# The first expert layer in quarters of the array's columns, with h turned in 32x32 squares on VectorE

## The chip, the cores and the metric

The kernel runs on one core of one Trainium2 chip. The metric is the device time of one execution in microseconds, as the median of several runs. The engines have short names in the profile: PE is TensorE (matmuls), PEld its weight loads, DVE is VectorE, ACT is ScalarE, POOL is GpSimd, SP is SyncE. PSUM is the memory that matmuls write to, SBUF the one they read from.

## What is computed

The first part is attention in chunks of 64, over 8 batches of 8 heads with 576 tokens of 64 numbers; the change does not touch it. Its output is seen as x with N = 4608 rows (tokens) of D = 512 numbers. Then each token goes to one of E = 8 experts, and this is where the change lies:

```python
xn = x / (np.linalg.norm(x, axis=-1, keepdims=True) + 1e-06)
en = expert_emb / (np.linalg.norm(expert_emb, axis=-1, keepdims=True) + 1e-06)
logits = xn @ en.T / tau
expert_idx = np.argmax(logits, axis=1)
...   # gate_w: the softmax weight of the chosen expert
for e in range(E):
    mask = expert_idx == e
    ...
    h = np.maximum(x[mask] @ w1[e], 0.0)          # 512 -> 1024
    out[mask] = gate_w[mask, None] * (h @ w2[e])  # 1024 -> 512
```

Everything is fp32.

## The kernel before

After attention and routing, the tokens are sorted by expert and worked through in steps of 128. A step holds two groups of G = 64 tokens, and each group (`s` = 0, 1) belongs to one expert, with weights of its own in SBUF (`w1_sb[s]`, `w2_sb[s]`, two buffers each). There are NT = 36 steps that always run, and up to 4 more under a condition, of which one runs with this input.

A matmul contracts over the 128 partitions: `lhsT` is loaded into the array, `rhs` streams past it, and the output lies in PSUM with one partition for each column of `lhsT`. A `lhsT` of 64 columns fills half of the array's columns, so the two groups run beside each other in the two halves. The name `tile(..., tag=..)` takes a buffer from a pool; a pool has `bufs` buffers for each tag, and a new tile of that tag waits until the last reader of the tile that had the buffer is done. The instructions of an engine are issued in the order of the program (`manual_schedule`).

```python
P, CH, G = 128, 64, 64; KD = D // P      # 4
KF = F // P                              # 8
ctx.enter_context(tc.manual_schedule())
...
with (
    tc.tile_pool(name="blk", bufs=2) as bp,
    tc.tile_pool(name="ps_x", bufs=1, space=PSUM) as ps_x,
    tc.tile_pool(name="ps_h", bufs=3, space=PSUM) as ps_h,
    tc.tile_pool(name="ps_ht", bufs=2, space=PSUM) as ps_ht,
    tc.tile_pool(name="ps_y", bufs=2, space=PSUM) as ps_y,
):
    ...

def turn_xb(j):
    t = xin.pop(j)
    ps = ps_x.tile([P, KD, P], FP32, tag="x", name="x_ps")
    for c in range(KD):
        nc.tensor.transpose(ps[:, c], t[:, c * P : c * P + P], ident)
    xT = bp.tile([P, KD, P], FP32, tag="xbT", name="xbT")
    nc.vector.tensor_copy(xT, ps)
    mo[j] = {"xT": xT, "xin": t}

def hidden(j):
    d = mo[j]
    h = bp.tile([P, F], FP32, tag="h", name="h")
    for fh in range(F // 512):
        ps = ps_h.tile([P, 512], FP32, tag="h", name="h_ps")
        for c in range(KD):
            for s in range(2):
                nc.tensor.matmul(
                    ps[G * s : G * s + G],
                    lhsT=d["xT"][:, c, G * s : G * s + G],
                    rhs=w1_sb[s][j % 2][:, c, fh * 512 : fh * 512 + 512],
                    start=(c == 0),
                    stop=(c == KD - 1),
                )
        dst = h[:, fh * 512 : fh * 512 + 512]
        if fh % 2:
            nc.scalar.activation(dst, ps, AF.Relu)
        else:
            nc.vector.tensor_scalar(dst, ps, 0.0, None, ALU.max)
    d["h"] = h

def turn_h(j):
    d = mo[j]
    hT = bp.tile([P, KF, P], FP32, tag="hT", name="hT")
    for g in range(KF // 4):
        ps = ps_ht.tile([P, 4, P], FP32, tag="ht", name="ht_ps")
        for c in range(4):
            f0 = (4 * g + c) * P
            nc.tensor.transpose(ps[:, c], d["h"][:, f0 : f0 + P], ident)
        if g % 2:
            nc.scalar.copy(hT[:, 4 * g : 4 * g + 4], ps)
        else:
            nc.vector.tensor_copy(hT[:, 4 * g : 4 * g + 4], ps)
    d["hT"] = hT

def result(j):
    d = mo.pop(j)
    ps = ps_y.tile([P, D], FP32, tag="y", name="y_ps")
    for c in range(KF):
        for s in range(2):
            nc.tensor.matmul(
                ps[G * s : G * s + G],
                lhsT=d["hT"][:, c, G * s : G * s + G],
                rhs=w2_sb[s][j % 2][:, c],
                start=(c == 0),
                stop=(c == KF - 1),
            )
    y = bp.tile([P, D], FP32, tag="y", name="y", bufs=3)
    nc.scalar.activation(y, ps, AF.Copy, scale=d["gate"])
    ...   # y goes to its rows of out by an indirect DMA
```

`hidden` makes h with tokens on the partitions and the 1024 features along the row. The second layer contracts over features, so it needs h turned, with features on the partitions: `turn_h` does this with eight 128x128 transposes on TensorE into PSUM, and two copies to SBUF give `hT`. `gates(j)` (not shown) makes the gate weight on ScalarE and VectorE. The order of the steps is this:

```python
load_w1(0)
load_w1(1)
load_w2(0)
load_w2(1)
turn_xb(0)
hidden(0)
load_w1(2)
gates(0)
turn_xb(1)
gates(1)

LEAST = NT
for j in range(LEAST + 1):
    if j + 1 < LEAST:
        hidden(j + 1)
        if j + 3 < NST:
            load_w1(j + 3)
    if j < LEAST:
        turn_h(j)
    if j + 2 < LEAST:
        turn_xb(j + 2)
        gates(j + 2)
    if j > 0:
        result(j - 1)
        if j + 1 < NST:
            load_w2(j + 1)
    if j + XBUF < NST:
        gather_x(j + XBUF)
        if j + XBUF + 1 < NST:
            gather_spot(j + XBUF + 1)

steps = number(n_steps, NST, ENG.PE, ENG.DVE, ENG.Activation, ENG.Pool, ENG.SP)

def more(j):
    with tc.If(steps > j):
        turn_xb(j)
        hidden(j)
        if j + 2 < NST:
            load_w1(j + 2)
        turn_h(j)
        gates(j)
        result(j)
        if j + 2 < NST:
            load_w2(j + 2)
        if j + 1 < NST:
            more(j + 1)

more(LEAST)
```

## Time and profile before

| | before |
|---|---|
| time, median of 3 runs | 806.37 us (802.37 to 807.18) |
| span of the profiled execution | 810.2 us |
| TensorE busy | 743.9 us, 92% of the span |
| ScalarE, VectorE busy | 290.7 us (36%), 251.7 us (31%) |
| h matmuls (L635) | 1184 records, 267.9 us busy |
| y matmuls (L668) | 1184 records, 262.0 us busy |
| turning of h (L656) | 296 records, 40.6 us busy |
| turning of x (L604) | 148 records, 22.8 us busy |

The profile shows one execution. An fp32 matmul leaves two records, so a step has 32 records for 16 h matmuls; 37 steps make 1184. The page cuts the span into 40 slices, each with a digit for the busy share of an engine in tenths; PEclk is the clock that TensorE was granted, in tenths of full speed. A group's line has the source line, the engine, the operation, output and inputs with their shapes, the count, then busy time and mean length of one in ns, then the idle time of the engine before them and what ended it. Attention and routing take up the first 200 us or so, and the expert steps run from about 210 us to the end.

### The profile page before, as it was taken

What the parts mean: (1) busy time and instruction counts of PE and PEld (TensorE: products, weight loads), DVE (VectorE), ACT (ScalarE), POOL (GpSimd) and SP (SyncE); (2) the same over time, 40 slices, a digit from 0 to 9 for tenths busy, and PEclk for the clock granted to TensorE, in tenths of its full rate; (3) what the DMA queues carried; (4) which work ended last, traced back from release to release, by engine and by line L of the source; (5) the groups of instructions that cost most, each with busy time, mean ns of one, the idle gap of its engine ahead of it and who ended that gap; (6) DMA issues with size and microseconds to landing.
All of it is one profiled execution on the core that took longest, in us unless ns stands there. A gap on an engine that the chain in (4) does not pass through costs nothing.

```text
span 810.2 us, 15342 instructions
## 1 busy us (share of the span) xinstructions
PE 743.9 (92%) x6033; PEld 367.7 (45%) x6033; DVE 251.7 (31%) x703; ACT 290.7 (36%) x520; POOL 221.3 (27%) x270
## 2 busy tenths in 40 slices
PE   2799999985569999999999999999999999999994
PEld 2688888874124333343343333343333343333331
DVE  2467777775221121121121121121121122122100
ACT  3345455441142243243243243333334334334102
POOL 4235556545420211211211311311211221221220
PEclk9999999995778999999999999999999999999998
DMA  9999999993670100115583416688530444312140
GB/s 177 234 264 246 238 251 234 258 399 133 233 247 1 51 27 27 53 59 202 189 305 131 155 61 229 253 328 323 169 118 27 144 144 131 140 44 79 72 150 9
DMA packets 117739, 132.37 MB, mean 163 GB/s; under 512 B 79860, under 2 KB 83252, under 8 KB 117664
## 3 DMA queue, kind: packets, MB, share of 16 engines
q1 hardware_dynamic: 101136, 84.18, 35.9%
q0 software_dynamic: 16528, 47.17, 18.4%
q8 instruction: 49, 0.80, 0.4%
q14 instruction: 26, 0.21, 0.1%
HBM read 383.07 MB, written 21.80 MB: 500 GB/s over the span
## 4 chain that ended last, share of the span: by engine, by line
PE 83%; DMA 4%; issue 3%; DVE 3%; SPq 3%; POOL 1%; ACT 0%; POOLq 0%; DVEq 0%; ACTq 0%
PE y_ps L668 31%; PE h_ps L635 29%; PE ht_ps L656 4%; PE rt_ps L288 4%; PE pv L255 3%; PE tr L280 3%; PE tr L199 3%; PE sc L215 2%; SPq L188 2%; PE tr L241 2%; PE x_ps L604 2%; DMA w<-in_moe_w_dram 2%; DMA spot<-spots,src_row 1%; DVE x L266 1%; SPq L176 1%
## 5 line engine op out<-in xcount | busy, mean ns | idle before, releaser
L635 PE MATMUL h_ps<-w,xbT 128*64 128x512 f32 x1184 | 267.9, 604 | 9.9 <-DMA w<-in_moe_w_dram 6.6
L668 PE MATMUL y_ps<-w,hT 128*64 128x512 f32 x1184 | 262.0, 595 | 0.0
L635 PEld LDWEIGHTS h_ps<-w,xbT 128*64 128x64 f32 x1184 | 88.5, 140 | 181.3 <-issue 174.4
L677 POOL DMA_INDIRECT out_dram<-y,spot x37 | 37.8, 1022 | 441.6 <-ACT y L676 425.7
L668 PEld LDWEIGHTS y_ps<-w,hT 128*64 128x64 f32 x1184 | 81.8, 137 | 154.6 <-issue 154.1
L644 ACT ACTIVATE h<-h_ps 128x512 f32<-128x512 f32 x37 | 22.1, 597 | 259.2 <-PE h_ps L635 231.8
L646 DVE TENSOR_SCALAR h<-h_ps 128x512 f32<-128x512 f32 x37 | 25.6, 691 | 225.4 <-PE h_ps L635 225.4
L676 ACT ACTIVATE y<-y_ps,gate 128x512 f32<-128x512 f32 x37 | 25.4, 687 | 126.1 <-PE y_ps L668 126.1
L660 DVE COPY hT<-ht_ps 128x512 f32<-128x512 f32 x37 | 25.6, 692 | 126.9 <-PE ht_ps L656 123.5
L623 ACT ACT_TABLE_LOAD x37 | 47.5, 1283 | 0.7
L618 ACT ACT_TABLE_LOAD x37 | 47.5, 1283 | 0.7
L527 POOL DMA_INDIRECT xin<-x_rows,spot x40 | 41.4, 1034 | 22.2 <-issue 11.3
L656 PEld LDWEIGHTS ht_ps<-ident,h 128*128 128x128 f32 x296 | 31.7, 141 | 30.4 <-issue 29.2
L282 ACT COPY xT<-tr 128x512 f32<-128x512 f32 x36 | 21.1, 586 | 64.8 <-PE tr L280 46.1
L527 POOL DMA_INDIRECT spot<-spots,src_row x40 | 40.4, 1009 | 13.9 <-issue 11.6
L288 PE MATMUL rt_ps<-enT,xT 128*128 128x8 f32 x288 | 37.6, 257 | 5.8 <-DVE m L310 5.7
L199 PE MATMUL tr<-ident,kx 128*128 128x128 f32 x144 | 24.2, 296 | 18.4 <-DMA kx<-in_k_dram 18.4
L288 PEld LDWEIGHTS rt_ps<-enT,xT 128*128 128x128 f32 x288 | 37.5, 203 | 7.7 <-DVE m L310 4.1
L656 PE MATMUL ht_ps<-ident,h 128*128 128x128 f32 x296 | 40.6, 280 | 0.1
L176 POOL DMA_DIRECT2D qx<-in_q_dram x40 | 35.3, 886 | 19.0 <-PE tr L199 17.8
L372 POOL DMA_INDIRECT spots<-m,dest x36 | 36.7, 1019 | 11.4 <-issue 10.6
L273 POOL DMA_DIRECT2D x_rows<-x x36 | 20.3, 565 | 70.0 <-DVE x L266 55.8
(123 smaller groups left out, 659.3 us busy)
## 6 DMA issues: line engine op xcount, KB each, us to landing
w<-in_moe_w_dram SPq DMA_DIRECT2D x160, 2048.0 KB
v<-in_v_dram SPq DMA_DIRECT2D x64, 144.0 KB
x_rows<-x POOLq DMA_DIRECT2D x36, 256.0 KB
qx<-in_q_dram POOLq DMA_DIRECT2D x32, 256.0 KB
kx<-in_k_dram SPq DMA_DIRECT2D x32, 256.0 KB
w<-in_moe_w_dram POOLq DMA_DIRECT2D x4, 2048.0 KB
spots<-empty SPq DMA_DIRECT2D x1, 2312.0 KB
qx<-in_q_dram POOLq DMA_DIRECT2D x8, 128.0 KB
```

The lines of the kernel that those rows point to most:

```text
L176: eng.dma_start(out=x[done : done + n], in_=src[b, :, s : s + n, :].rearrange("h p d -> p h d"),)
L199: nc.tensor.transpose(ps[:, i], a[:, i * P : i * P + P], ident)
L288: nc.tensor.matmul(rt_ps[:, 0, batch_of[t][1]], lhsT=d["xT"][:, c], rhs=enT[:, c], start=(c == 0), stop=(c == KD - 1),)
L372: ins = nc.gpsimd.indirect_dma_start(out=spots, out_offset=bass.IndirectOffsetOnAxis(ap=at, axis=0), in_=m, in_offset=None, bounds_check=S ...
L527: nc.gpsimd.indirect_dma_start(out=dst, out_offset=None, in_=table, in_offset=bass.IndirectOffsetOnAxis(ap=at, axis=0), bounds_check=rows - 1,
L618: nc.scalar.activation(rn, rn, AF.Sqrt)
L623: nc.scalar.activation(sh, sh, AF.Exp, accum_out=gate)
L635: nc.tensor.matmul(ps[G * s : G * s + G], lhsT=d["xT"][:, c, G * s : G * s + G], rhs=w1_sb[s][j % 2][:, c, fh * 512 : fh * 512 + 512], sta ...
L646: nc.vector.tensor_scalar(dst, ps, 0.0, None, ALU.max)
L656: nc.tensor.transpose(ps[:, c], d["h"][:, f0 : f0 + P], ident)
L668: nc.tensor.matmul(ps[G * s : G * s + G], lhsT=d["hT"][:, c, G * s : G * s + G], rhs=w2_sb[s][j % 2][:, c], start=(c == 0), stop=(c == KF ...
L677: ins = nc.gpsimd.indirect_dma_start(out=out, out_offset=bass.IndirectOffsetOnAxis(ap=spot[:, j, E : E + 1].bitcast(I32), axis=0), in_=y, ...
```

## The change

It makes h in another arrangement, so that the turning for the second layer needs no TensorE. A transpose on VectorE turns 32x32 squares, each in its place: of a square of 32 partitions by 32 elements, rows become columns, but the square does not move to other partitions. So h has to lie such that each square is already on the partitions that its features need. The new `hidden` takes 32 tokens at a time as `lhsT`, in one of four quarters of the array's columns. Quarter `r` (32 columns) computes, for these 32 tokens, the features whose number modulo 128 lies in 32r to 32r + 31: it reads w1 in pieces of 32 columns, one from each 128. Its output is on partitions 32r to 32r + 31. Each square then holds 32 tokens by 32 features on the partitions where hT wants those features, and one VectorE transpose for each half of the tokens writes hT. Relu is done by ScalarE alone on the way from PSUM to SBUF.

A step has 64 matmuls of 256 columns in place of 16 of 512 columns, and no transposes or copies for h. `turn_h` goes; its work stands at the end of `hidden`. PSUM buffers that it used go to x (2 in place of 1) and h (4 in place of 3). The buffers of the SBUF tiles stay as they were: two each for `xbT`, `h` and `hT`, where an `h` tile now holds half a step.

```diff
--- before.py
+++ after.py
@@ -46,6 +46,7 @@
     NT = N // P
     NCB = S // CH
     G = P // 2
+    Q = 32
     NST = NT + E // 2
     scale = 1.0 / float(Dh) ** 0.5
     XBUF = 4
@@ -562,9 +563,8 @@
 
     with (
         tc.tile_pool(name="blk", bufs=2) as bp,
-        tc.tile_pool(name="ps_x", bufs=1, space=PSUM) as ps_x,
-        tc.tile_pool(name="ps_h", bufs=3, space=PSUM) as ps_h,
-        tc.tile_pool(name="ps_ht", bufs=2, space=PSUM) as ps_ht,
+        tc.tile_pool(name="ps_x", bufs=2, space=PSUM) as ps_x,
+        tc.tile_pool(name="ps_h", bufs=4, space=PSUM) as ps_h,
         tc.tile_pool(name="ps_y", bufs=2, space=PSUM) as ps_y,
     ):
         def number(ap, top, *engines):
@@ -626,38 +626,31 @@
             d["gate"] = gate
 
         def hidden(j):
-            d = mo[j]
-            h = bp.tile([P, F], FP32, tag="h", name="h")
-            for fh in range(F // 512):
-                ps = ps_h.tile([P, 512], FP32, tag="h", name="h_ps")
-                for c in range(KD):
-                    for s in range(2):
-                        nc.tensor.matmul(
-                            ps[G * s : G * s + G],
-                            lhsT=d["xT"][:, c, G * s : G * s + G],
-                            rhs=w1_sb[s][j % 2][:, c, fh * 512 : fh * 512 + 512],
-                            start=(c == 0),
-                            stop=(c == KD - 1),
-                        )
-                dst = h[:, fh * 512 : fh * 512 + 512]
-                if fh % 2:
-                    nc.scalar.activation(dst, ps, AF.Relu)
-                else:
-                    nc.vector.tensor_scalar(dst, ps, 0.0, None, ALU.max)
-            d["h"] = h
-
-        def turn_h(j):
+
+
+
             d = mo[j]
             hT = bp.tile([P, KF, P], FP32, tag="hT", name="hT")
-            for g in range(KF // 4):
-                ps = ps_ht.tile([P, 4, P], FP32, tag="ht", name="ht_ps")
-                for c in range(4):
-                    f0 = (4 * g + c) * P
-                    nc.tensor.transpose(ps[:, c], d["h"][:, f0 : f0 + P], ident)
-                if g % 2:
-                    nc.scalar.copy(hT[:, 4 * g : 4 * g + 4], ps)
-                else:
-                    nc.vector.tensor_copy(hT[:, 4 * g : 4 * g + 4], ps)
+            for s in range(2):
+                w = w1_sb[s][j % 2].rearrange("p c (k r i) -> p c r k i", r=P // Q, i=Q)
+                ps = ps_h.tile([P, G // Q, KF * Q], FP32, tag="h", name="h_ps")
+                for b in range(G // Q):
+                    t0 = G * s + Q * b
+                    for c in range(KD):
+                        for r in range(P // Q):
+                            nc.tensor.matmul(
+                                ps[Q * r : Q * r + Q, b].rearrange("p (k i) -> p k i", i=Q),
+                                lhsT=d["xT"][:, c, t0 : t0 + Q],
+                                rhs=w[:, c, r],
+                                start=(c == 0),
+                                stop=(c == KD - 1),
+                            )
+                h = bp.tile([P, G // Q, KF * Q], FP32, tag="h", name="h")
+                nc.scalar.activation(h, ps, AF.Relu)
+                nc.vector.transpose(
+                    hT[:, :, G * s : G * s + G].rearrange("p k (b i) -> p b k i", i=Q),
+                    h.rearrange("p b (k i) -> p b k i", i=Q),
+                )
             d["hT"] = hT
 
         def result(j):
@@ -702,8 +695,6 @@
                 hidden(j + 1)
                 if j + 3 < NST:
                     load_w1(j + 3)
-            if j < LEAST:
-                turn_h(j)
             if j + 2 < LEAST:
                 turn_xb(j + 2)
                 gates(j + 2)
@@ -724,7 +715,6 @@
                 hidden(j)
                 if j + 2 < NST:
                     load_w1(j + 2)
-                turn_h(j)
                 gates(j)
                 result(j)
                 if j + 2 < NST:
```

## The prediction

> **What bounds the kernel now.** I read the shares by engine first, then the slices, then the chain that ended last, then one step of the expert stage in order of time.

> ```profile
> PE 743.9 (92%) x6033; PEld 367.7 (45%) x6033; DVE 251.7 (31%) x703; ACT 290.7 (36%) x520; POOL 221.3 (27%) x270
> PE   2799999985569999999999999999999999999994
> PE 83%; DMA 4%; issue 3%; DVE 3%; SPq 3%; POOL 1%; ACT 0%; POOLq 0%; DVEq 0%; ACTq 0%
> ```

> TensorE is busy for 92% of the span, and 83% of the chain lies on it. From slice 14 on there is no hole. That part is the expert loop, which the change touches. The chain in the window from 414 to 446 us gives the loop's period:

> ```profile
> 414.26 6.87 PE h_ps L635 x32
> 421.13 1.02 PE ht_ps L656 x8
> 422.15 0.44 PE x_ps L604 x4
> 422.59 7.02 PE y_ps L668 x32
> 429.61 6.87 PE h_ps L635 x32
> ```

> A step is 6.87 + 1.02 + 0.44 + 7.02 = 15.35 us, all on TensorE. No other engine ends a wait of it. So a microsecond taken from TensorE's step is a microsecond gained, provided nothing new makes TensorE wait. The timeline shows how the others lie beside it:

> ```profile
> 421.75 0.69 DVE L660 COPY hT<-ht_ps 128x512 f32<-128x512 f32 x1 [3.32 <-PE ht_ps L656]
> 422.63 0.69 DVE L606 COPY xbT<-x_ps 128x512 f32<-128x512 f32 x1 [0.18 <-PE x_ps L604]
> 423.24 0.15 DVE L619 TENSOR_REDUCE lmax<-spot 128x1 f32<-128x8 f32 x1
> 429.44 7.04 PE L635 MATMUL h_ps<-w,xbT 128*64 128x512 f32 x32
> 429.68 0.69 ACT L676 ACTIVATE y<-y_ps,gate 128x512 f32<-128x512 f32 x1 [3.16 <-PE y_ps L668]
> ```

> xbT, which the next h needs, is ready at 423.3, six microseconds before that h starts at 429.44. ScalarE starts on y 0.24 us after TensorE has gone on to h: that is how long the last y matmul takes to reach another engine. VectorE starts its next instruction 0.61 us after a copy of 0.69 us started (422.63 to 423.24), so a queue of such operations costs 0.61 us each and 0.69 us for the last.

> [...]
> 1. [...] the order on VectorE (hT, xbT, lmax) is the program's order in every step I looked at.
> 2. [...]
> 3. [...] 4 transposes after transposes take 0.44 us, so 8 should take 0.88, but the 8 that follow h take 1.02. y after the transposes takes 7.02, h after y 6.87. A change costs about 0.15 us.
> 4. [...] here the half follows windows that are only partly idle:

> ```profile
> 28.70:32.10 3.40, 1.51 (x64) 1.21 (x57) 2.74 (x6) 1.12 (x3) 0.96 (x2) 1.00 1.36 198
> 32.10:35.60 3.50, 3.09 (x41) 2.67 (x42) 0.71 (x2) 0.58 (x1) 1.31 (x2) 0.51 1.13 253
> ```

> (Columns: stretch, length, busy PE, weight loads, DVE, ACT, POOL, then granted clock.) 1.51 us of busy in 3.4 was followed by a window at 0.51.

> **The change, part by part.**

> *Removed from TensorE:* the turning of h, 1.02 us a step. But h now runs in 32-column tiles and x in the whole array, so h to x is a change of mode that the turning of h paid before: +0.15. Net -0.87.

> *The h matmuls themselves.* Before: 16 matmuls of 512 columns, two records each, two at a time, so 16 pairs at 6.87 / 16 = 0.429 us. After: 64 matmuls of 256 columns, 128 records, four at a time, so 32 groups. By the column a group costs half of 0.429, 0.215, and 32 of them 6.87 us: no gain and no loss. Will four run at once, with four weight loads hidden? Attention already has such a case, in 64x64 tiles:

> ```profile
> 80.65 0.69 PE L215 MATMUL sc<-kxT,qxT 64*64 64x64 f32 x32
> L215 PE MATMUL sc<-kxT,qxT 64*64 64x64 f32 x1152 | 26.8, 233 | 1.2 <-issue 1.2
> ```

> 32 records end in 0.69 us of which the last takes 0.23, so 8 groups of four start within about 0.46: 58 ns a group, for 64 columns that cost 54 at the rate above (0.429 / 512). Four at once does work, weight loads and issue included, and here each group has 0.215 us to hide them in. I take 6.87. The stretched read of w1 (32 columns, then a jump) and four streams from the same 128 rows are not shown by this trace.

> *ScalarE:* two Relus of 512 in place of a Relu and a copy (0.60 + 0.59 before): the same. *VectorE:* out go a Relu and a copy of 0.69 each, in come two transposes of 512. Its operations on about that many fp32 elements take 0.69 to 0.74 here, from PSUM or from SBUF (128x560 from SBUF: 0.74), [...].

> *What moves, and this decides it.* The hT tile keeps two buffers. Before, hT(j) was written after h(j+1), when result(j-2) had already been issued: a buffer was free. Now hidden(j+1) writes hT(j+1) before result(j-1) is issued, while hT(j-1) is still to be read by result(j-1) and hT(j) by result(j). Three live tiles, two buffers. So both transposes of hT(j+1) wait on VectorE until the last matmul of result(j-1). Behind them in VectorE's queue stands the copy of xbT(j+2), and the very next thing TensorE does after result(j-1) is hidden(j+2), which needs xbT(j+2). The copy that was six microseconds early comes late. TensorE idles for: 0.24 (last y matmul seen elsewhere) + 0.61 + 0.61 (two transposes) + 0.69 (xbT) + about 0.05 (from xbT's end to the matmul) + 0.06 (a first matmul with unhidden weights: the first y takes longer by that) = 2.26. I take 2.3.

> *Step after:* 6.87 + 0.15 + 0.44 + 7.02 + 2.3 = 16.78, against 15.35: +1.43 us. The wait stands before hidden(3) to hidden(35), 33 times: +47. At the end, where no xbT follows, the removed turning of h is gained in the last whole steps and in the conditional one: about -1.4.

> *The clock.* A window of 3.4 us that holds a whole gap has some 1.1 us of work in it, less than the 1.51 above, so I expect the next window at half now and then, costing half of it, 1.7 us. Gap and window drift against each other by 16.78 - 5 x 3.413 = -0.28 us a step, and a half window shifts the phase by 1.4 the other way, so this repeats perhaps every sixth to eighth step: about five times, +8 (an estimate with wide margins).

> Sum: 806.4 + 47 - 1.4 + 8 = 860 us.

> **The rivals.**
> - *The wait isn't there* (the buffer is free in time, or xbT slips ahead). Then 36 steps gain 0.87 us: 806.4 - 31 = 775. For it: nothing else in the loop is near the limit. Against it: two buffers, program order[...]. I give it one in fifteen.
> - *The quarter tiles don't run at full rate* (four streams of w1, jumps of 512 bytes, 256 records a step). At 10% slower, 0.7 us a step, +25: 885; at half rate, over 1100. For it: no such case in the trace. Against it: the 58 ns groups.
> - *The transpose is slower than a copy.* At twice 0.69 the gap grows by 1.4 us a step, +46, with more half windows: about 920. [...]
> - *A cheaper gap and a clock that stays full:* 2.1 us, no half windows: 846.

> **Range and chances.** The centre is the sum, 860. Below it lie the shorter gap without the clock (846) and some unseen overlap, above it the clock's worst case (a half window every second step, +20) and slightly slower quarters (+25). 838 to 900 should hold it 8 times in 10. All but the first rival are slower, so faster 0.06, same 0.03, slower 0.91.

> **What would show it.** Right: in the chain's window h still about 6.87 for 128 records, no ht_ps, a TensorE wait of 2.2 to 2.4 us before each h put down to VectorE's xbT, the transposes waiting for y_ps, and slices with PEclk under 9 in the loop. Wrong: h starting directly after y (775), h above 7.2 (the quarter tiles), transposes over 0.8 us (VectorE's rate), or a full clock in all slices.

## The result, and the profile after

The changed kernel takes 857.6 us (median; 855.3 to 858.4), the kernel before on the same chip 804.6 us (802.4 to 807.2). The ratio is 1.065 [1.061, 1.070]: slower by 53.0 us. The prediction was 860, that is 53.6 us slower than its 806.4.

The page of the changed kernel: shares by engine, TensorE's slices, the granted clock, the chain by engine, and the group of the transposes. In the group's line 48.6 is busy time in us, 692 the mean of one in ns, 497.7 the idle time before them in us, with what ended most of it.

```profile
PE 718.1 (84%) x9289; PEld 422.7 (49%) x9289; DVE 241.9 (28%) x703; ACT 286.1 (33%) x520; POOL 221.7 (26%) x270
...
PE   2699999955499989998999899989988999899994
...
PEclk9899999976899999999999999999999999999998
...
PE 76%; issue 11%; DMA 5%; DVE 3%; SPq 2%; POOL 1%; ACT 0%; POOLq 0%; DVEq 0%
...
L650 DVE STREAM_TRANSPOSE hT<-h 128x512 f32<-128x512 f32 x74 | 48.6, 692 | 497.7 <-PE y_ps L661 475.4
```

TensorE's busy time fell from 743.9 to 718.1 us: the removed work is really gone. But its share fell from 92% to 84%, eights stand between the nines of the expert loop, and 11% of the chain is "issue" where it was 3%. The transposes take 0.69 us each and wait 475 us for the matmuls of y (L661), which do not write anything that a transpose reads.

The chain through two steps of the changed kernel (start, length, what):

```profile
423.11 7.11 PE h_ps L641 x128
430.23 0.59 PE x_ps L604 x4
430.81 7.02 PE y_ps L661 x32
437.83 2.12 issue
439.95 7.11 PE h_ps L641 x128
```

h, x and y stand as before, without the turning of h. New is a hole of 2.12 us between y and h. The step is 7.11 + 0.59 + 7.02 + 2.12 = 16.84 us. The timeline shows what fills the hole:

```profile
437.98 1.30 DVE L650 STREAM_TRANSPOSE hT<-h 128x512 f32<-128x512 f32 x2 [13.59 <-PE y_ps L661]
439.20 0.65 DVE L606 COPY xbT<-x_ps 128x512 f32<-128x512 f32 x1
...
439.95 7.11 PE L641 MATMUL h_ps<-w,xbT 128*32 128x256 f32 x128 [2.12 <-issue]
```

y ends at 437.83. VectorE has idled for 13.59 us, starts the two transposes at 437.98, the copy of xbT at 439.20, and h starts 0.10 us after that copy's end. The transposes' inputs were there long before (h's matmuls ended at 430.2, the Relu on ScalarE at 430.9); what they wait for is y's last matmul, which frees the buffer that they write to. The chain calls the hole "issue", because the trace shows no wait of that matmul for the copy; only the timeline gives the order of events.

The start of the 4th h to the start of the 36th takes 491.0 us in the trace before and 544.3 after: 53.3 more in 32 steps. That is the whole of the difference. (The spans of the two traces, 810.2 and 855.4, lie only 45.2 apart because the part ahead of the loop took 7.2 us longer in the traced execution of the kernel before: its 2nd h starts at 224.2, that of the changed kernel at 217.0.)

### The profile page after: what moved, and what is told of

Its sections match the earlier page's. It is cut to its first block, busy times and chain, and to the rows that moved or that the text cites. A ratio compares the mean times of both kernels' runs of the same rounds, so it can differ in the third digit from the quotient of the medians.

```text
span 855.4 us, 21956 instructions
## 1 busy us (share of the span) xinstructions
PE 718.1 (84%) x9289; PEld 422.7 (49%) x9289; DVE 241.9 (28%) x703; ACT 286.1 (33%) x520; POOL 221.7 (26%) x270
## 4 chain that ended last, share of the span: by engine, by line
PE 76%; issue 11%; DMA 5%; DVE 3%; SPq 2%; POOL 1%; ACT 0%; POOLq 0%; DVEq 0%
PE y_ps L661 29%; PE h_ps L641 29%; PE rt_ps L289 3%; PE tr L200 3%; PE sc L216 3%; PE x_ps L604 2%; PE pv L256 2%; PE tr L281 2%; DMA w<-in_moe_w_dram 2%; PE tr L242 2%; DMA kx<-in_k_dram 2%; SPq L189 1%; DMA spot<-spots,src_row 1%; DVE mx L224 1%; DVE a L226 1%
## 5 line engine op out<-in xcount | busy, mean ns | idle before, releaser
L641 PE MATMUL h_ps<-w,xbT 128*32 128x256 f32 x4736 | 275.1, 392 | 83.6 <-issue 70.5
L641 PEld LDWEIGHTS h_ps<-w,xbT 128*32 128x32 f32 x4736 | 181.4, 113 | 189.8 <-issue 118.5
L661 PE MATMUL y_ps<-w,hT 128*64 128x512 f32 x1184 | 262.8, 595 | 0.5 <-DVE lmax L619 0.5
L650 DVE STREAM_TRANSPOSE hT<-h 128x512 f32<-128x512 f32 x74 | 48.6, 692 | 497.7 <-PE y_ps L661 475.4
L661 PEld LDWEIGHTS y_ps<-w,hT 128*64 128x64 f32 x1184 | 82.1, 137 | 156.8 <-issue 155.4
L649 ACT ACTIVATE h<-h_ps 128x512 f32<-128x512 f32 x74 | 44.2, 597 | 228.5 <-PE h_ps L641 228.5
L623 ACT ACTIVATE sh<-sh 128x8 f32<-128x8 f32 x37 | 7.7, 209 | 206.1 <-DVE sh L622 206.0
L528 POOL DMA_INDIRECT xin<-x_rows,spot x40 | 41.4, 1036 | 21.8 <-issue 11.3
L528 POOL DMA_INDIRECT spot<-spots,src_row x40 | 40.3, 1008 | 13.9 <-issue 11.6
L604 PE MATMUL x_ps<-ident,xin 128*128 128x128 f32 x148 | 24.7, 290 | 13.0 <-DMA xin<-x_rows,spot 13.0
L205 DVE COPY qxT<-tr 128x512 f32<-128x512 f32 x36 | 24.7, 687 | 22.2 <-PE tr L200 20.3
```

The lines of the kernel that those rows point to most:

```text
L528: nc.gpsimd.indirect_dma_start(out=dst, out_offset=None, in_=table, in_offset=bass.IndirectOffsetOnAxis(ap=at, axis=0), bounds_check=rows - 1,
L623: nc.scalar.activation(sh, sh, AF.Exp, accum_out=gate)
L641: nc.tensor.matmul(ps[Q * r : Q * r + Q, b].rearrange("p (k i) -> p k i", i=Q), lhsT=d["xT"][:, c, t0 : t0 + Q], rhs=w[:, c, r], start=(c ...
L649: nc.scalar.activation(h, ps, AF.Relu)
L650: nc.vector.transpose(hT[:, :, G * s : G * s + G].rearrange("p k (b i) -> p b k i", i=Q), h.rearrange("p b (k i) -> p b k i", i=Q),)
L661: nc.tensor.matmul(ps[G * s : G * s + G], lhsT=d["hT"][:, c, G * s : G * s + G], rhs=w2_sb[s][j % 2][:, c], start=(c == 0), stop=(c == KF ...
```

## The experiments

The theory: three live hT tiles share two buffers, the transposes stand in VectorE's queue until y's last matmul has read the oldest, and xbT, which the next h needs, is queued behind them. The rivals: the quarter tiles or the transposes themselves are slow, or the clock. Where a ratio follows, it is to the kernel before, timed on the same chip. The runs were on three chips, on which the kernel before took 803, 813 and 813 to 814 us; this turns out to matter.

**A third hT buffer.** Nothing else changes, so the wait must go.

```diff
-            hT = bp.tile([P, KF, P], FP32, tag="hT", name="hT")
+            hT = bp.tile([P, KF, P], FP32, tag="hT", name="hT", bufs=3)
```

> The changed kernel with a third buffer for hT, nothing else. If the wait for a free hT buffer is the cause: the transposes no longer wait for y, xbT is early again, and TensorE goes from y to h with only a change of mode (0.15 us). A step falls from 16.84 to about 14.70 us (h 6.90 + skew 0.05, two changes and x 0.74, y 6.86, one more change 0.15), 33 times 2.14 = 71 us less, and the three half-clock windows go too (5 us): about 782 us, 0.97 of the kernel before. If turning h on VectorE is on the path by itself (h, Relu, transposes, y as one chain): the step stays at about 16.8 and the time at 855 to 858.

Measured: 829.4 us, ratio 1.022 [1.018, 1.026]. In the chain h now starts where y ends:

```profile
426.01 7.02 PE y_ps L661 x32
433.03 4.53 PE h_ps L641 x74
```

The wait before h is gone, but 17 us over the kernel before remain (829.4 - 812.6): h itself is now slow in its middle (8.2 us in place of 7.1). The expectation was missed; why is the matter of the last part of this section.

**The transposes behind xbT in the queue.** Two buffers as in the changed kernel, but `turn_h` is a function again and is called after the next x has been copied, so that the transposes may wait without holding xbT up.

```diff
-                nc.vector.transpose(hT[:, :, ...], h...)      # in hidden(j)
+        def turn_h(j): ...                                    # both transposes of hT(j)
...
             if j + 2 < LEAST:
                 turn_xb(j + 2)
+            if j + 1 < LEAST:
+                turn_h(j + 1)
+            if j + 2 < LEAST:
                 gates(j + 2)
```

> The changed kernel with two hT buffers as it is, but with the transposes put behind the copy of xbT in VectorE's queue. If the cause is the order in the queue behind a wait: the transposes still wait for the last y matmul, but nothing that TensorE needs stands behind them; step 14.70, about 782 us, as with three buffers. If the shortage of buffers costs by itself, whatever stands behind it in the queue: the wait before h stays, 850 or more, and the two kernels differ.

Measured: 830.1 us, 1.021 [1.018, 1.024]. The transposes wait for y as before, yet TensorE has no hole between y and h (two lines of the chain, then the first transpose from the timeline):

```profile
428.52 7.02 PE y_ps L667 x32
435.54 6.74 PE h_ps L640 x114
435.68 0.71 DVE L656 STREAM_TRANSPOSE hT<-h 128x512 f32<-128x512 f32 x1 [6.43 <-PE y_ps L667]
```

So not the transposes' wait costs the time, but what stands behind them. Here too h has the slow middle, some ten groups later than with three buffers, and the 782 us that were expected are missed again. (A group is the four matmul records that run at once in the four quarters; h has 32.)

**The kernel before with one hT buffer.** If the shortage of buffers is the cause, it must do the same without quarter tiles and without VectorE's transposes.

```diff
-            hT = bp.tile([P, KF, P], FP32, tag="hT", name="hT")
+            hT = bp.tile([P, KF, P], FP32, tag="hT", name="hT", bufs=1)
```

> The kernel before with one hT buffer in place of two: the same shortage without quarter tiles and without VectorE transposes. If the wait is the whole mechanism: hT's copy waits for the last y matmul, xbT stands behind it, and TensorE waits before each h for about 0.3 + 0.61 + 0.65 + 0.1 = 1.7 us, 33 or 34 times: 804.6 + 57 = about 861 us, with a full clock, since the gap is shorter. If the loss belongs to the transposes or the quarter tiles: about 805 us, as before.

Measured: 869.3 us, 1.071 [1.066, 1.076], 56.8 us more than the kernel before, where 57 were expected; the step is 16.98 in place of 15.34. Its timeline:

```profile
430.82 0.69 DVE L660 COPY hT<-ht_ps 128x512 f32<-128x512 f32 x1 [11.25 <-PE y_ps L668]
431.43 0.68 DVE L606 COPY xbT<-x_ps 128x512 f32<-128x512 f32 x1
...
432.16 5.37 PE L635 MATMUL h_ps<-w,xbT 128*64 128x512 f32 x24 [1.42 <-DVE xbT L606]
```

The same pattern with one instruction in front of xbT in place of two: hT's copy waits for y, xbT is behind it, h waits for xbT. This is the theory without any part of the change in it.

**Each transpose twice.** The second writes the same again, so only VectorE's part of the hole grows.

```diff
-                nc.vector.transpose(hT[:, :, ...], h...)
+                for _ in range(2):
+                    nc.vector.transpose(hT[:, :, ...], h...)
```

> The changed kernel with each VectorE transpose issued twice (the second writes the same values again), two hT buffers. If the transposes lie in the wait: 2 x 0.61 = 1.22 us more a step, 33 times, +40, and a gap of 3.4 us that empties most of a clock window often, each half window another 1.7 us (10 to 30 of them, +12 to +45): 910 to 945 us. If they lie beside other work: no change, about 858.

Measured: 962.3 us, 1.183 [1.179, 1.187]; the chain:

```profile
414.60 7.02 PE y_ps L662 x32
421.62 3.62 issue
425.24 8.89 PE h_ps L641 x128
```

The hole grew by 3.62 - 2.12 = 1.50 us for two more transposes, 0.75 each: VectorE's queue sets its length. The time is above the 910 to 945 us expected. The 1.50 in place of the 1.22 that were expected make 9 us in 33 steps; the kernel before takes 8 us longer on this chip than on that of the comparison (812.6 against 804.6); and the half clock came about as often as the upper end had it: 27 half windows in the 32 steps from the 4th h to the 36th, where the changed kernel has three (mean granted clock 0.917 against 0.964). h takes 8.9 us in such a step.

**The doubled transposes with three buffers.** The doubled work of the last run and the third buffer of the first. If the transposes' own time counts, it shows here.

> Three hT buffers and each VectorE transpose issued twice (the second writes the same values again). If the transposes lie beside other work once a buffer is free: no change against three buffers alone, 1.02 of the kernel before, within half a per cent. If turning h on VectorE is still on a chain that sets the step: up to 1.2 us a step more, 40 us, 1.07.

Measured: 780.0 us, 0.972 [0.967, 0.978], with a step of 14.65 us. So VectorE has room for four transposes a step when they need not wait for y: xbT still stands behind them, and TensorE does not wait for it. The surprise is that h has no slow middle here, although this kernel does more than the first one. This run and the next two were on another chip than those above.

**The gathers moved from under h to under y.** Three hT buffers; GpSimd's gathers of the next x and spot (L528) get their x tile from a ring of two in place of four, so that they wait for the turning of x and are issued under y.

```diff
-            xin[j] = xin_sb[j % XBUF]
+            xin[j] = xin_sb[j % 2 if j < NT else 2 + j - NT]
...
             if j + 2 < LEAST:
                 turn_xb(j + 2)
                 gates(j + 2)
+            fetch(j + XBUF)      # gather_x(j + XBUF) and gather_spot(j + XBUF + 1)
             if j > 0:
                 result(j - 1)
...
-            if j + XBUF < NST:
-                gather_x(j + XBUF)
-                if j + XBUF + 1 < NST:
-                    gather_spot(j + XBUF + 1)
```

> Three hT buffers, and the two gathers of a step (a row of spots, 128 rows of x) wait until x of two steps on has been read, so that GpSimd issues them under y and not under h. With three buffers h takes 7.9 us from its first to its last record in place of 6.7: three groups of four come 0.5 to 0.7 us apart, always about the time in which GpSimd issues the gathers (0.1 to 1.7 us after their starts, in both kernels without the wait). If the gathers or their data cause it: h back to 6.74, a step of 14.7 us, 38 us less than with three buffers, about 0.975 of the kernel before. If they only stand beside it: h stays at 7.9, 1.02.

Measured: 772.4 us, 0.961 [0.958, 0.965], step 14.65 and no slow middle. The kernel before takes 803.5 on this chip. Of the 31 us between them, 22 lie in the 32 loop steps (491.0 to 468.8); from the 2nd to the 4th h it takes 25.4 us where the kernel before takes 36.5, which was not pursued.

**xbT copied only after y.** Three hT buffers, so that the transposes wait for nothing, but the copy of xbT is made to wait: VectorE first copies a column of the y that TensorE has just made.

```diff
+        def copy_xb(j, after=None):      # called after result(j - 3), with its y_ps as after
...
+                peek = bp.tile([P, 1], FP32, tag="peek", name="peek")
+                nc.vector.tensor_copy(peek, after[:, 0:1])
+            d["xT"] = bp.tile([P, KD, P], FP32, tag="xbT", name="xbT")
+            nc.vector.tensor_copy(d["xT"], d["x_ps"])
```

> Three hT buffers, but the copy of xbT is made to follow y: VectorE reads one column of y first. TensorE then waits about 1.1 us before each h, without any transpose in that wait. If the slow stretch within h comes from TensorE having no pause before h, in which its instructions can be made ready: h back to 6.74 us as in the changed kernel, a step of about 15.8, and a time equal to three buffers alone (1.02). If the slow stretch comes from the gathers whatever went before: h stays at 7.9, a step of about 16.9, 1.07.

Measured: 836.3 us, 1.041 [1.036, 1.045], step 16.37: 1.72 us more than the 14.65 of the two kernels above. The timeline:

```profile
433.13 0.16 DVE L611 COPY peek<-y_ps 128x1 f32<-128x1 f32 x1 [7.00 <-ACT y L675]
433.21 0.68 DVE L613 COPY xbT<-x_ps 128x512 f32<-128x512 f32 x1
...
433.99 2.37 PE L647 MATMUL h_ps<-w,xbT 128*32 128x256 f32 x40 [1.65 <-ACT junk L623]
```

A late xbT alone makes the hole, with hT free. The releaser named for h, ScalarE's junk, writes nothing that h reads; xbT ends at 433.89, 0.10 us before h starts. The hole is 1.65 us, not the 1.1 expected, so the time lies between the two forecasts. h has no slow middle, but none of the three kernels traced on this chip has one, so this run does not tell whether a pause before h takes it away.

**The slow middle of h.** What remained was why three buffers gave 1.02 on one chip and the same with doubled transposes 0.97 on another. The first two kernels and the moved gathers were run again together. This was the chip of the first four experiments, not another one as the first expectation says:

> The kernel of the first experiment once more, on another chip, beside the two others of this call. Theory A (the slow stretch inside h belonged to the chip or the moment, not to the kernel): no stretch this time, 32 groups of h at 215.6 ns, h about 7.05 us in the chain, step about 14.65 us as in the run with doubled transposes, and with 37 fewer transposes on VectorE nothing else changes: about 0.97 of the time before (778 if before is 803). Theory B (the stretch belongs to this kernel: GpSimd's gathers are issued under h, and the order of the loop puts them there): three or four groups of 480 to 690 ns near the 17th to 20th group of every step again, h about 8.2 us, step 15.8, about 1.02 of before.

> The kernel of the second experiment once more, on the same chip as the two others of this call. Theory A (chip or moment): no stretch in h, step about 14.65 us, 0.97 of before. Theory B (kernel): the stretch at the 26th to 30th group again, step 15.9, 1.02 of before. If this one has it and the three buffers' kernel does not, or the other way round, neither theory stands as it is.

> The kernel with the gathers moved under y once more, on the same chip as the two repeats. Theory A (chip or moment): if the chip of this call shows no stretch in the other two, this one is 0.961 of before again and the three lie within 1% or so of each other; if the chip does show it in the other two, this one tells whether moving the gathers takes it away (then the gathers are needed for it: 0.96) or moves it into y (then 1.02). Theory B (kernel): 0.96 here beside 1.02 for the two others.

Measured: 827.0, 829.8 and 782.2 us with the kernel before at 813.9, that is 1.016 [1.012, 1.020], 1.018 [1.013, 1.023] and 0.962 [0.957, 0.966]. On the same chip the slow middle is there with the gathers under h, and gone with them under y. The chain with three buffers:

```profile
434.85 4.43 PE h_ps L641 x74
439.29 0.05 issue
439.34 0.66 PE h_ps L641 x6
440.00 0.07 issue
440.07 2.83 PE h_ps L641 x48
```

and with the gathers moved:

```profile
425.42 7.04 PE h_ps L641 x128
432.46 0.59 PE x_ps L604 x4
433.05 7.02 PE y_ps L661 x32
```

7.04 us without a break against 8.05. The timeline of the first of the two shows when (PEld is TensorE's weight loads):

```profile
437.22 1.03 POOL L528 DMA_INDIRECT xin<-x_rows,spot  x1 [0.30 <-issue]
438.56 1.00 POOL L528 DMA_INDIRECT spot<-spots,src_row  x1 [0.31 <-issue]
438.61 0.19 PEld L641 LDWEIGHTS h_ps<-w,xbT 128*32 128x32 f32 x6 [0.23 <-issue]
439.35 0.16 PEld L641 LDWEIGHTS h_ps<-w,xbT 128*32 128x32 f32 x6 [0.55 <-issue]
440.08 2.34 PEld L641 LDWEIGHTS h_ps<-w,xbT 128*32 128x32 f32 x47 [0.57 <-issue]
```

While GpSimd issues the second gather, and for half a microsecond after it, TensorE's records come in lumps, six weight loads every 0.7 us, and the profile shows nothing that it waits for in between. With xbT first the gathers come 2.2 us later in h, and so does the slow stretch. But the doubled transposes with three buffers had their gathers at the same place in h, to 0.01 us, and no stretch. So they were run on a second chip, beside three buffers alone:

> Three buffers and doubled transposes once more, now beside the three-buffer kernel on the same chip. The slow stretch of h has so far been seen where the kernel before took 813 and 814 us (both runs of the three-buffer kernel and of the xbT-first kernel) and not where it took 803 (this kernel). Theory C (the chip and the gathers together): this kernel has no stretch of its own accord; it will show it (about 1.02 of before, step 15.8 us) if this chip is one of the slower ones, before near 813, and not (0.972, step 14.65) if before is near 803. Theory D (the second transposes take it away): no stretch on any chip, 0.972.

> The three-buffer kernel for the third time, beside the doubled transposes on the same chip. Theory C (the chip and the gathers together): the two kernels of this call do the same, both with the stretch (1.02) or both without (0.97), by whether before takes 813 or 803. Theory D (the kernel alone: gathers under h, unless the second transposes lie there): 1.02 here with the stretch at the 17th to 20th group, on any chip, and no stretch in the other.

Measured: 827.7 and 827.6 us, with the kernel before at 812.9: 1.017 [1.014, 1.021] and 1.018 [1.014, 1.021]. The kernel that had 0.972 has 1.017 here, and its h breaks as the other's does:

```profile
438.82 4.50 PE h_ps L641 x74
443.32 0.10 issue
443.42 0.66 PE h_ps L641 x6
```

So it takes two things: gathers under a quarter-tile h, and one of the chips that show it, here two of three. The doubled transposes have no part in it. That was shown; what differs between the chips was not found. A pause before h does not take it away either: the doubled transposes with two buffers ran on the first chip with the gathers under h, and the five h's between the 4th and the 36th that had the full clock take 7.94 to 8.05 us, each after a hole of 3.6 us or more. The kernel before with one hT buffer ran on one of the two chips, had its gathers under h as well, and none of its pairs in three steps took over 0.43 us but the first (0.48). A possible reading, an estimate from these records and not shown by a run: quarter tiles need 8 records of TensorE (4 weight loads, 4 matmuls) every 0.216 us, 37 a us; half tiles need 4 every 0.429, 9 a us; in the stretch 24 records come in 1.47 us (12 weight loads from 438.61 to 440.08, and their matmuls), 16 a us. A supply of 16 a us would starve the one and not the other.

## Why the prediction was right

**The wait.** This was the step that decided, and the runs bear it out: removed by a third buffer, removed by moving xbT ahead of the transposes, reproduced in the kernel before by one buffer less, and lengthened by 0.75 us for each transpose added. Its size was 2.26 by its terms. Measured: 0.15 from y's end to the transposes, 1.22 for two of them, 0.65 for xbT, 0.10 to h, in sum 2.12 by the chain; against the step of 14.65 without wait it costs 16.84 - 14.65 = 2.19.

**h at 6.87 and the change of mode.** The quarter tiles do run four at once: a group takes 0.2156 us where the prediction had 0.2147, with four weight loads hidden in each: the 128 loads of an h run from 439.92 for 6.66 us, beside its matmuls from 439.95 for 7.11. x takes 0.59 as predicted (0.44 + 0.15). The one term that was too small is h: 7.04 in the chain without wait, 0.17 over. 32 groups make 6.90. Most of the rest is a third change of mode that the prediction left out: y runs in 128x64 tiles and h now in 128x32, where before both had 128x64. The last pair of y and the first records of h, before and with the gathers moved:

```profile
429.01 0.60 PE L668 MATMUL y_ps<-w,hT 128*64 128x512 f32 x2
429.44 0.60 PE L635 MATMUL h_ps<-w,xbT 128*64 128x512 f32 x2
...
406.45 0.60 PE L661 MATMUL y_ps<-w,hT 128*64 128x512 f32 x2
406.98 0.42 PE L641 MATMUL h_ps<-w,xbT 128*32 128x256 f32 x4
```

From y's last pair to h it was 0.43 us and is 0.53, and the first group of h takes 0.24 in place of 0.216. So the step without wait is 14.65 and not 14.48, and the step with it 16.84 and not 16.78.

**The transposes.** They were taken to last as long as a copy, which no trace had shown. They take 692 ns each in the mean (668 to 712), with an output in strides. The copies of the same size to hT and xbT took 692 and 691 in the kernel before; xbT's takes 652 in the median here. Rival three (slow transposes) is out, and so is rival two (slow quarters) on the chip of the comparison.

**The clock.** Predicted were about five half windows, 8 us. There were four in the loop, and each cost 1.65 us, 6.6 in sum. One of them, with the window before it (columns as in the prediction):

```profile
503.86:507.27 3.41, 1.34 (x8) 0.17 (x4) 1.93 (x5) 0.00 (x0) 0.00 (x0) 1.00 0.01 5
507.27:510.68 3.41, 3.35 (x32) 1.85 (x36) 0.85 (x6) 0.88 (x3) 1.31 (x2) 0.50 0.04 11
```

1.34 us of work in a window, then half clock in the next. The four half windows begin at 387.80, 507.27, 660.87 and 797.40 us, each within 0.13 us of the start of an h, and each lasts 3.41 us. They lie 119.47, 153.60 and 136.53 us apart, 35.0, 45.0 and 40.0 times 3.413 us (409.60 / 120; the prediction took this figure with no trace to show it), that is 7, 9 and 8 steps (the prediction had every sixth to eighth). Every stretch of half clock between two of full clock, in this trace and in that of the kernel before, lasts one or more times 3.413 us, at 0.50 of the full clock. A window that ended 0.12 us before the start of an h stayed without effect:

```profile
776.90:780.31 3.41, 1.41 (x8) 0.24 (x4) 1.86 (x4) 0.00 (x0) 0.00 (x0) 1.00 0.00 0
780.31:783.72 3.41, 3.29 (x64) 2.44 (x68) 0.92 (x7) 0.88 (x3) 1.25 (x2) 1.00 0.00 0
```

With the edges of the windows counted in steps of 3.413 us from the drop at 387.80, the four ahead of the half windows hold 1.28 to 1.34 us of work, and all others from the 4th h to the 36th 1.39 or more. So the prediction's mark of 1.51, taken from attention, was too high for this loop. It served because a window that holds nearly the whole hole has 1.28 to 1.34 us of work.

**The sum.** 32 steps at +1.50 make 48 us and three of the half windows 5 (the fourth comes after them): 53.3. The steps ahead of these and the end give back 0.5 and 0.4, and from the 2nd h to the end it is 52.4 in the traces, 53.0 in the times. The estimate for the end was -1.4; without its half window it was -2.0. That the total came within 1 us is partly luck: h was taken 0.17 us a step too small and the wait 0.11 too large (2.3 against 2.19), and the 2 us that this leaves were made up by the half windows (6.6 us where 8 were predicted) and the end.

**The first rival**, no wait at 775 us, is what the change is worth where the wait is taken away: 780 (with doubled transposes) and 772 on the chip where h runs smoothly, though some 10 us of the 772 come from the start of the loop and not from the wait (35.3 us from the 2nd to the 4th h in the one, 25.4 in the other). Three buffers alone were not run there. On the two others the third buffer alone leaves it at 1.02 of the kernel before; with the gathers moved one of them has 782 where the kernel before takes 814, and on the other this was not run. The changed kernel itself was timed on the chip of the comparison alone; whether that is one of the three is not known.

## What to carry to other kernels

When a producer is moved ahead of the consumer that frees its buffer, count the live tiles again: three hT tiles on two buffers made a hole of 2.12 us in each step here. VectorE took its instructions in the order of the program (the transposes at 437.98, xbT at 439.20), so the wait was paid by what stood behind it, here a copy that had been six microseconds early. One buffer more, or the urgent instruction ahead in the queue, took the hole away (1.022 and 1.021 of the kernel before in place of 1.065), and both are worth trying before the change itself is given up. A kernel with as many small matmuls as this one should be compared on more than one chip (the doubled transposes with three buffers had 0.972 on one and 1.017 on another), and other engines' gathers tried away from its densest stretch (782 us in place of 827 on one chip).
